# Attention and the first token products issued from one written list of small steps; q's decay table and the identity made on the chip

## The chip, the cores and the metric

The kernel runs on one core of one Trainium2 chip. The metric is the time of one execution on the device in microseconds (us), the median of three runs. A profiled execution of the same program gives the trace; its times are counted from its first instruction.

## What is computed

Three layers follow each other. Only the first and the beginning of the second are touched by the change. The shapes are batch 2, 8 heads, 768 tokens, head size 64, model width 512.

```
# attention with decay, per batch and head
for t in range(768):
    state = gamma[h] * state + outer(k[t], v[t])
    y[t]  = scale * q[t] @ state
x = y with the heads side by side            # [2, 768, 512]

# second layer
theta = x @ w_theta
zr, zi = x * cos(theta), x * sin(theta)
u = x + einsum("ts,bsd->btd", w_tok_r, zr) + einsum("ts,bsd->btd", w_tok_i, zi)
x = u + relu(u @ w_ch)

# third layer: a token MLP (w_tok1, w_tok2) and a channel MLP (w_ch1, w_ch2), each with relu and a residual
```

The weights come as float64 and are turned into float32 on the chip.

## The kernel before

**Tiling.** The 768 tokens are six chunks of 128 (c = 0 to 5), for two batches (b = 0, 1). All tiles are 128 partitions by 512 floats (256 KiB) and come from one list of 82 slots in on-chip memory.

**Attention of a chunk.** `scores(b, c)` multiplies k and q (tiles kT, qT) into banks 0 to 3 of PSUM on TensorE (PE). `masked` multiplies these by the decay mask on VectorE (DVE): two instructions to each batch, into tiles A. `intra` multiplies A by v (tile kv) into two banks of 4, 5 and 6; it opens the bank's sums with b = 0. `inter` adds q with its decay (qs) times the state. `decayed` makes qs from qT and the table qtab, and ks from k (another kv tile) and the table tabs, one DVE instruction each. `keep_x` copies the result out of PSUM on ScalarE (ACT): a rounded half xh, and the exact x into the tile X. `rest` subtracts xh in PSUM with a matrix `minus` (a negated identity), and ACT copies the remainder xl. `grow` adds ks times v to the state's sums in bank 7, and `spread` scales them into the next state on ACT.

**Weights.** `Weights` converts a 512 KiB tile in three steps. `begin` is two short DVE instructions on the loaded tile (raw) and one on ACT. `join` is one DVE instruction and one on ACT (wh). `end` is one DVE instruction (wl). Four raw tiles are in flight: a `join` sends for the next load. `theta_part(b, c, j)` is three matmuls of 128x512 with one quarter of w_theta; four of them make a theta tile. `angle`, `sines` and `turned` make cos and sin of theta on ACT and DVE, turn X on PE against the identity, and multiply and split (zh, zl). `tok(b, s, ...)` adds token chunk s to all the sums: 24 matmuls of 128x512, and 24 of 128x256.

**Order.** The program is in manual order: each engine runs its instructions in the order in which the code issues them. All loads go through the queue of SyncE (SP). Attention runs chunk by chunk (`attend`, `summed`). The theta products of chunks 0 to 2 of batch 0 stand between the scores and the intra products of chunk 4, with the conversion steps of w_theta. Chunks 4 and 5 of q, k and v are loaded behind w_theta and two tiles of w_tok. Then a loop over n = 0 to 11 does, for each (b, s), `tok` and the preparation of later tiles.

Of the kernel before, what the change touches and what calls it, by code (L numbers as in the profile page):

```python
# [8 lines left out]
F32 = mybir.dt.float32  # L9
# [46 lines left out]
            self.free_ids.append(i)  # L56


@with_exitstack
def body(ctx, tc, qk, kv, mask, tabs, qtab, ident_in, w_theta, w_tok, w_ch, w_tok1, w_tok2, w_ch1, w_ch2, out):  # L60
    nc = tc.nc
    NCH = 6
    const = ctx.enter_context(tc.tile_pool(name="const", bufs=1))
# [16 lines left out]
    def warm(n):  # L80

        for i in range(n):
            o = banks[7].rearrange("p (a b) -> p a b", a=4)
            nc.tensor.matmul(o, still, still.unsqueeze(1).to_broadcast([P, 4, P]), start=True, stop=True)
# [6 lines left out]
    magic = const.tile([P, 1], F32, name="magic")  # L91
    minus = const.tile([P, P], F32R, name="minus")

    X = const.tile([P, 3, 4, W], F32, name="X")
    nc.gpsimd.memset(half_pi, math.pi / 2)
    nc.gpsimd.memset(magic, MAGIC)

# [100 lines left out]
            return self.done[i : i + n]  # L198


    raw_t = {}

    def load_qk(b, c, parts=1):
        t = [sl.get(F32, n) for n in ("qT", "kT")]
        for i in range(parts):
            pp = slice(i * W // parts, (i + 1) * W // parts)
            for j in range(2):
                nc.sync.dma_start(out=t[j][:, pp], in_=qk[b, c, j][:, pp])  # L208
        raw_t[b, c] = t

    def load_kv(b, c, j):
        t = sl.get(F32, "kv")
        nc.sync.dma_start(out=t, in_=kv[b, c, j])
        raw_t[b, c].insert(2 + 2 * j, t)

    def load_att(b, c):
        load_qk(b, c)
        for j in range(2):
            load_kv(b, c, j)

    xs, z = {}, {}
    S, A, Q, K, V, Y, PS, R = {}, {}, {}, {}, {}, {}, {}, {}
    YS = [4, 5, 6]
    halves = [slice(64 * half, 64 * half + 64) for half in range(2)]

    def scores(b, c):

        qT, kT = raw_t[b, c][:2]
        ps = S[b, c] = banks[2 * b : 2 * b + 2]
        for p in range(4):  # L230
            pp = slice(p * P, (p + 1) * P)
            for half, r in enumerate(halves):
                nc.tensor.matmul(ps[half][:, pp], kT[r, pp], qT[r, pp], start=True, stop=True)  # L233
        let_go(b, c)

    def let_go(b, c):

        if (b, c) in V:
            sl.put(*raw_t.pop((b, c))[:3])
        else:  # L240
            V[b, c] = raw_t[b, c][3]

    def masked(b, c):
        A[b, c] = []
        for ps, m in zip(S.pop((b, c)), mask_sb):
            at = sl.get(F32, "A")
            nc.vector.tensor_mul(at, ps, m)
            A[b, c].append(at)

    def decayed(b, c):  # L250

        qT, _, k, _ = raw_t[b, c]
        if c:
            qs = sl.get(F32, "qs")
            nc.vector.tensor_mul(qs, qT, qtab_sb)
            Q[b, c] = qs
        if c < NCH - 1:
            ks = sl.get(F32, "ks")
            k3 = k.rearrange("p (h d) -> p h d", h=8)
            kt = tabs_sb[:, c, 0:8].unsqueeze(2).to_broadcast([P, 8, 64])  # L260
            nc.vector.tensor_mul(ks.rearrange("p (h d) -> p h d", h=8), k3, kt)
            K[b, c] = ks
        let_go(b, c)

# [11 lines left out]
    def third(c):  # L278

        return next(i for i in YS if all(banks[i] is not y for y in chunk(c)))  # L280
# [16 lines left out]
    def intra(b, c):  # L297
        y, a, v = chunk(c), A.pop((b, c)), V[b, c]
        for p in (0, 2, 1, 3):
            for half in range(2):  # L300
                i, ro, cc = place(b, p, half)
                hh = slice((2 * p + half) * 64, (2 * p + half + 1) * 64)
                first = b == 0 and p < 2
                nc.tensor.matmul(y[i][ro, cc], v[:, hh], a[half][:, p * P : (p + 1) * P], start=first, stop=True, skip_group_check=True)
        sl.put(*a)
# [14 lines left out]
    def rest(c):  # L320

        for i in range(2):
            hi, y = xs[c][i]
            nc.tensor.matmul(y, minus, hi, start=False, stop=True, skip_group_check=True)  # L324
            lo = sl.get(name="xl")
            nc.scalar.copy(lo, y)
            xs[c][i] = hi, lo
# [32 lines left out]
    def theta(b, c, wt, to):  # L360

        for j in range(4):
            theta_part(b, c, j, wt[j], to)
# [441 lines left out]
        nc.sync.dma_start(out=mask_sb[i], in_=mask[:, i].rearrange("p a t -> p (a t)"))  # L805
    for b in BOTH:
        load_kv(b, 0, 1)
    for b in BOTH:
        load_qk(b, 1)
    nc.sync.dma_start(out=tabs_sb, in_=tabs)  # L810
    for b in BOTH:
        load_kv(b, 0, 0)
    nc.sync.dma_start(out=ident, in_=ident_in)
    for b in BOTH:
        load_kv(b, 1, 1)
    nc.sync.dma_start(out=qtab_sb, in_=qtab)
    for b in BOTH:
        load_kv(b, 1, 0)
    for c in (2, 3):
        for b in BOTH:  # L820
            load_qk(b, c)
        for b in BOTH:
            for j in range(2):
                load_kv(b, c, j)
    for _ in range(4):
        ws.fetch()
    scores(0, 0)
    scores(1, 0)
    warm(6)
    for b in BOTH:  # L830
        masked(b, 0)
    intra(0, 0)
    warm(1)
    intra(1, 0)

    def attend(c, first, then, last):

        keep_x(c)
        first()
        for b in BOTH:  # L840
            decayed(b, c + 1)
            scores(b, c + 1)
        for b in BOTH:
            masked(b, c + 1)
        then()
        rest(c)
        grow(c)
        spread(c)
        last()

    def summed(c):
        for b in BOTH:
            intra(b, c)
        inter(c)

    def nothing():
        pass

    keep_x(0)
    for b in BOTH:  # L860
        scores(b, 1)
    for b in BOTH:
        decayed(b, 0)
    for b in BOTH:
        masked(b, 1)
    nc.scalar.activation(out=minus, in_=ident, func=AF.Copy, scale=-1.0)
    rest(0)
    grow(0)
    spread(0)
    for b in BOTH:  # L870
        decayed(b, 1)
    summed(1)
    attend(1, nothing, nothing, nothing)
    for b in BOTH:
        load_att(b, 4)
    summed(2)
    attend(2, nothing, nothing, lambda: ws.begin())
    ws.begin()
    ws.join()
    summed(3)  # L880
    ws.begin()
    ws.join()
    ws.end()
    attend(3, nothing, nothing, lambda: ws.begin())
    for b in BOTH:
        load_att(b, 5)
    for j in range(4):
        for i in range(3):
            theta_part(0, i, j, ws.done[j], (3, 2, third(4))[i])
            if j == 3:  # L890
                angle(0, i)
        if j < 2:
            ws.join()
        if j < 3:
            ws.end()
        if j == 1:
            ws.begin()
        if j == 2:
            ws.join()
            ws.begin()  # L900
            ws.end()
    wth = ws.done[0:4]
    sines(0, 0)
    summed(4)
    attend(4, nothing, nothing, nothing)
    turned(0, 0, third(5))
    ws.join()
    ws.begin()
    ws.end()
    summed(5)  # L910
    keep_x(5)
    theta(0, 3, wth, 7)
    sines(0, 1)
    ws.join()
    wtok = {0: ws.take(TOK, 3)}
    sl.put(*mask_sb, *state, qtab_sb)
    rest(5)
    grow(5)
    ws.begin()
    angle(0, 3)  # L920
    turns = [(b, c) for b in BOTH for c in range(NCH)]

    for n, (b, s) in enumerate(turns):
        tok(b, s, wtok[s], range(0, 4))
        if n:
            if n < 11:
                sines(*turns[n + 1])
            if n + 1 < NCH:
                wtok[n + 1] = ws.take(TOK + 3 * n + 3, 3)
        else:  # L930
            ws.join()
            ws.begin()
        if n < 11:
            turned(*turns[n + 1], 7)
        if n < 8:
            theta(*turns[n + 4], wth, 6)
        tok(b, s, wtok[s], range(4, 8))
        if n < 8:
            angle(*turns[n + 4])
        if n == 7:  # L940
            for x in wth:
                sl.put(*x)
        if n == 0:
            wtok[1] = ws.take(TOK + 3, 3)
        if n == NCH - 1:
            evac_u(0)
        if b:
            for x in wtok[s]:
                sl.put(*x)
            ws.pump((3, 3, 2, 2, 4, 2)[s])  # L950
        if n == 10:
            split_x(0)
# [103 lines left out]
    down_both()  # L1056


_INS = ["qk", "kv", "mask", "tabs", "qtab", "ident", "w_theta", "w_tok", "w_ch", "w_tok1", "w_tok2", "w_ch1", "w_ch2"]


def _order():
# [8 lines left out]
def _layout(q, k, v, moe_w_theta, moe_w_tok_r, moe_w_tok_i, moe_w_ch, moe2_w_tok1, moe2_w_tok2, moe2_w_ch1, moe2_w_ch2):  # L1071
# [27 lines left out]
    st = st[:, None].repeat(D, axis=1).reshape(P, n, 4)  # L1099
    arr["tabs"] = np.concatenate([kt, st], axis=2).astype(np.float32)  # L1100

    qt = (gamma[:, None] ** t[None, :] * scale).reshape(4, 2, P).transpose(1, 0, 2)
    arr["qtab"] = np.ascontiguousarray(qt[:, None].repeat(D, axis=1).reshape(P, W)).astype(np.float32)
    arr["ident"] = np.eye(P, dtype=np.float32)

    def two(a, b):

# [32 lines left out]
```

## Time and profile before

| | |
|---|---|
| median of three runs | 450.27 us (450.26 to 450.79) |
| the profiled execution | 451.72 us, span 449.9 us |
| mean granted TensorE clock | 0.992 of full speed |
| PE busy | 438.0 us of the span, 97% |
| DVE busy | 352.0 us, 78% |
| ACT busy | 228.8 us, 51% |

PE is busy nearly always, but the mean hides where it is not. The first 45 us have most of its idle time, and the one stretch in which the clock is below full speed. A time in the trace that stands in square brackets is the idle time of the engine ahead of that row, with what ended it.

### The profile page before, as it was taken

What the parts mean: (1) busy time and instruction counts of PE and PEld (TensorE: products, weight loads), DVE (VectorE), ACT (ScalarE), POOL (GpSimd) and SP (SyncE); (2) the same over time, 40 slices, a digit from 0 to 9 for tenths busy, and PEclk for the clock granted to TensorE, in tenths of its full rate; (3) what the DMA queues carried; (4) which work ended last, traced back from release to release, by engine and by line L of the source; (5) the groups of instructions that cost most, each with busy time, mean ns of one, the idle gap of its engine ahead of it and who ended that gap; (6) DMA issues with size and microseconds to landing.
All of it is one profiled execution on the core that took longest, in us unless ns stands there. A gap on an engine that the chain in (4) does not pass through costs nothing.

```text
span 449.9 us, 7132 instructions
## 1 busy us (share of the span) xinstructions
PE 438.0 (97%) x2668; PEld 367.3 (82%) x2668; DVE 352.0 (78%) x648; ACT 228.8 (51%) x411; POOL 0.3 (0%) x6
## 2 busy tenths in 40 slices
PE   7897999999999999999999999999999999999997
PEld 4775878788888888888888888888888888888886
DVE  2688776888826678899976699999878997777892
ACT  1565686677633556545534245557534545566110
POOL 0000000000000000000000000000000000000000
PEclk9996999999999999999999999999999999999999
DMA  8999512544400232374541513678220002978022
GB/s 274 385 395 390 183 48 95 176 172 142 159 8 0 95 138 96 107 255 134 204 142 45 190 60 99 228 246 265 87 94 0 2 0 70 364 269 281 0 95 93
DMA packets 36034, 68.46 MB, mean 152 GB/s; under 512 B 4128, under 2 KB 15776, under 8 KB 36000
## 3 DMA queue, kind: packets, MB, share of 16 engines
q1 hardware_dynamic: 35424, 67.10, 43.1%
q10 hardware_dynamic: 576, 0.92, 0.6%
q8 instruction: 21, 0.34, 0.3%
q14 instruction: 13, 0.11, 0.1%
HBM read 53.84 MB, written 14.16 MB: 151 GB/s over the span
## 4 chain that ended last, share of the span: by engine, by line
PE 86%; DMA 8%; ACT 2%; DVE 2%; issue 1%; SPq 1%; ACTq 0%
PE bank L112 28%; PE bank L113 28%; PE bank L114 27%; DMA kT<-in_qk 4%; DMA kv<-in_kv 2%; DMA raw<-in_w_theta 2%; PE bank L459 1%; PE bank L385 1%; PE bank L339 1%; SPq L208 1%; PE bank L324 0%; PE bank L233 0%; DVE ta L370 0%; ACT X L317 0%; ACT xh L312 0%
## 5 line engine op out<-in xcount | busy, mean ns | idle before, releaser
L113 PE MATMUL bank<-wl,zh 128*128 128x512 f32 (+1 forms) x192 | 64.9, 338 | 0.5 <-DVE wl L176 0.5
L112 PE MATMUL bank<-wh,zh 128*128 128x512 f32 (+1 forms) x192 | 64.8, 338 | 0.0
L114 PE MATMUL bank<-wh,zl 128*128 128x512 f32 (+1 forms) x192 | 64.6, 336 | 0.0
L144 ACT ACTIVATE f<-raw 128x512 f32<-128x512 f32 x56 | 37.5, 679 | 34.7 <-DVE raw L143 31.2
L154 DVE SCALAR_TENSOR_TENSOR f<-f,raw 128x512 uint32<-128x512 uint32 x56 | 38.4, 685 | 6.4 <-ACT f L144 6.4
L113 PEld LDWEIGHTS bank<-wl,zh 128*128 128x128 f32 x192 | 36.4, 190 | 4.9 <-DVE wl L176 1.3
L112 PEld LDWEIGHTS bank<-wh,zh 128*128 128x128 f32 x192 | 36.4, 190 | 3.8
L114 PEld LDWEIGHTS bank<-wh,zl 128*128 128x128 f32 x192 | 36.4, 189 | 3.8
L112 PE MATMUL bank<-uh,wh 128*128 128x512 f32 x96 | 37.4, 390 | 0.0
L113 PE MATMUL bank<-ul,wh 128*128 128x512 f32 x96 | 37.4, 389 | 0.0
L114 PE MATMUL bank<-uh,wl 128*128 128x512 f32 x96 | 37.4, 389 | 0.0
L113 PE MATMUL bank<-gl,a 128*128 128x512 f32 (+1 forms) x90 | 33.7, 375 | 0.0
L114 PE MATMUL bank<-gh,a 128*128 128x512 f32 (+1 forms) x90 | 33.7, 375 | 0.0
L112 PE MATMUL bank<-gh,a 128*128 128x512 f32 (+1 forms) x90 | 33.7, 375 | 0.0
L112 PE MATMUL bank<-bh,ah 128*128 128x512 f32 x84 | 32.7, 389 | 0.0
L113 PE MATMUL bank<-bl,ah 128*128 128x512 f32 x84 | 32.7, 389 | 0.0
L114 PE MATMUL bank<-bh,al 128*128 128x512 f32 x84 | 32.7, 389 | 0.0
L161 ACT CAST wh<-f 128x512 fp32r<-128x512 f32 x28 | 17.4, 622 | 15.4 <-DVE f L154 15.2
L143 DVE TENSOR_SCALAR raw<-raw 128x512 f32<-128x512 f32 x56 | 23.5, 420 | 2.2 <-DMA raw<-in_w_ch 2.0
L388 DVE TENSOR_TENSOR tb<-bank,tb 128x512 f32<-128x512 f32 x12 | 8.3, 689 | 20.3 <-PE bank L385 13.8
L145 DVE TENSOR_SCALAR raw<-raw 128x512 uint32<-128x512 uint32 x56 | 23.6, 422 | 0.0
L176 DVE TENSOR_TENSOR wl<-f,wh 128x512 fp32r<-128x512 f32 x28 | 19.3, 689 | 3.8 <-ACT wh L161 3.2
(132 smaller groups left out, 984.7 us busy)
## 6 DMA issues: line engine op xcount, KB each, us to landing
raw<-in_w_ch SPq DMA_DIRECT2D x28, 512.0 KB, 4.2
raw<-in_w_tok SPq DMA_DIRECT2D x24, 512.0 KB, 3.8
kv<-in_kv SPq DMA_DIRECT2D x24, 256.0 KB, 5.8
a<-keep_s SPq DMA_DIRECT2D x24, 256.0 KB, 5.3
a<-keep_a SPq DMA_DIRECT2D x18, 256.0 KB, 4.8
keep_s<-ah SPq DMA_DIRECT2D x24, 128.0 KB, 1.8
keep_s<-al SPq DMA_DIRECT2D x24, 128.0 KB, 1.8
qT<-in_qk SPq DMA_DIRECT2D x11, 256.0 KB, 5.8
```

Of the source, the lines that this page charges most:

```text
L112: nc.tensor.matmul(o, ah, bh, start=first, stop=False, skip_group_check=True)
L113: nc.tensor.matmul(o, ah, bl, start=False, stop=False, skip_group_check=True)
L114: nc.tensor.matmul(o, al, bh, start=False, stop=last, skip_group_check=True)
L143: nc.vector.tensor_scalar(out=upper, in0=upper, scalar1=MOST, scalar2=-MOST, op0=ALU.min, op1=ALU.max)
L144: nc.scalar.activation(out=f, in_=upper, func=AF.Prelu, scale=REBIAS, alpha=-SIGN)
L145: nc.vector.tensor_scalar(out=lower, in0=lower, scalar1=29, scalar2=None, op0=ALU.logical_shift_right)
L154: nc.vector.scalar_tensor_tensor(out=fu, in0=fu, scalar=3, in1=lower, op0=ALU.logical_shift_left, op1=ALU.bitwise_or)
L161: nc.scalar.copy(h, f)
L176: nc.vector.tensor_sub(l, f, h)
L208: nc.sync.dma_start(out=t[j][:, pp], in_=qk[b, c, j][:, pp])
L339: nc.tensor.matmul(o, ks[:, hh], v[:, hh], start=(b == 0 and c == 0 and p == 0), stop=True, skip_group_check=True)
L388: nc.vector.tensor_mul(u, pn, u)
```

## The change

1. A table `ORDER` of small steps (one batch of one chunk each) replaces the chunk functions, the theta block and the first three turns of the loop: attention, conversion steps, theta products and `tok` for token chunks 0 to 2 stand in it. The loop starts at turn `BEGUN` = 3. The theta products now stand behind the last attention product.
2. `decayed` becomes `decayed_q` and `decayed_k`, which are placed apart.
3. The loads stand ahead of all work, in another order. All of chunk 4 comes before w_theta. Two tiles of w_theta come before chunk 5 and two behind it. k of chunk 5 in its natural layout, which nothing reads, isn't loaded.
4. The table qtab (256 KiB) isn't loaded. Two rows of 128 and 512 floats (qrow) come through ACT's queue, one matmul spreads them over 128 partitions into bank 7, and ACT copies the result.
5. The identity (64 KiB) isn't loaded. GpSimd (POOL) makes it with a memset and a select.
6. Of seven fill matmuls on a zero tile (`warm`) beside the first scores two stay.

```
+ORDER = [
+    ('mk', 0, 0), ('ia', 0, 0), ('mk', 1, 0), ('ia', 1, 0), ('sc', 0, 1), ('dq', 0, 1), ('dk', 0, 0), ('kx', 0),
...
+    ('j',), ('an', 1, 0),
+]
+BEGUN = 3
...
+    qrows = [sl.get(F32, "qrow") for _ in range(2)]
+    nc.scalar.dma_start(out=qrows[0][0:2, 0:P], in_=qtab[:, 0:P])
+    nc.scalar.dma_start(out=qrows[1][0:2], in_=qtab[:, P:])
...
+    nc.gpsimd.memset(ident, 0.0)
+    nc.gpsimd.affine_select(
+        out=ident, in_=ident, compare_op=ALU.not_equal, fill=1.0, base=0, pattern=[[-1, P]], channel_multiplier=1
+    )
...
+    def decayed_q(b, c):
+        qs = Q[b, c] = sl.get(F32, "qs")
+        nc.vector.tensor_mul(qs, raw_t[b, c][0], qtab_sb)
+        read(b, c)
+
+    def decayed_k(b, c):
+        k, ks = KN.pop((b, c)), sl.get(F32, "ks")
...
-    for b in BOTH:
-        load_qk(b, 1)
+    load_qk(0, 1)
     nc.sync.dma_start(out=tabs_sb, in_=tabs)
     for b in BOTH:
         load_kv(b, 0, 0)
-    nc.sync.dma_start(out=ident, in_=ident_in)
-    for b in BOTH:
-        load_kv(b, 1, 1)
-    nc.sync.dma_start(out=qtab_sb, in_=qtab)
-    for b in BOTH:
-        load_kv(b, 1, 0)
-    for c in (2, 3):
+    load_qk(1, 1)
+    for j in (1, 0):
+        for b in BOTH:
+            load_kv(b, 1, j)
+    for c in range(2, NCH):
+        if c == NCH - 1:
+            ws.fetch()
+            ws.fetch()
         for b in BOTH:
             load_qk(b, c)
-        for b in BOTH:
-            for j in range(2):
+        for j in (1, 0) if c < NCH - 1 else (1,):
+            for b in BOTH:
                 load_kv(b, c, j)
-    for _ in range(4):
-        ws.fetch()
+    ws.fetch()
+    ws.fetch()
...
+    steps = dict(
+        sc=scores, mk=masked, dq=decayed_q, dk=decayed_k, ia=intra, ir=inter, kx=keep_x, re=rest, gr=grow, sp=spread,
+        b=ws.begin, j=ws.join, e=ws.end, an=angle, si=sines, tu=turned, tk=token, wa=warm,
+        th=lambda b, c, j, to: theta_part(b, c, j, wth[j], to),
+    )
     scores(0, 0)
+    nc.scalar.activation(out=minus, in_=ident, func=AF.Copy, scale=-1.0)
     scores(1, 0)
-    warm(6)
...
+    warm(2)
+    nc.tensor.matmul(banks[7], qrows[0][0:2, 0:P], qrows[1][0:2], start=True, stop=True)
+    nc.scalar.copy(qtab_sb, banks[7])
+    sl.put(*qrows)
+    for name, *args in ORDER:
+        steps[name](*args)
...
-    for n, (b, s) in enumerate(turns):
+    wtok[BEGUN] = ws.take(TOK + 3 * BEGUN, 3)
+    for n, (b, s) in list(enumerate(turns))[BEGUN:]:
         tok(b, s, wtok[s], range(0, 4))
...
```

How the instructions stand now is seen at three places. The first is SP's queue around the loads of w_theta. Before, where qT_435 is q of chunk 4 in batch 0 and qT_671 that of chunk 5:

```order
L119 DMA raw<-in_w_theta 128x1024 x4
L208 DMA qT_435<-in_qk 128x512
L208 DMA kT_436<-in_qk 128x512
L213 DMA kv_439<-in_kv 128x512
L213 DMA kv_441<-in_kv 128x512
L208 DMA qT_443<-in_qk 128x512
L208 DMA kT_444<-in_qk 128x512
L213 DMA kv_447<-in_kv 128x512
L213 DMA kv_449<-in_kv 128x512
L119 DMA raw<-in_w_tok 128x1024 x2
L208 DMA qT_671<-in_qk 128x512
L208 DMA kT_672<-in_qk 128x512
```

Now, where kv_233 and kv_235 are k of chunk 4 and qT_241 is q of chunk 5 in batch 0:

```order
L249 DMA kv_233<-in_kv 128x512
L249 DMA kv_235<-in_kv 128x512
L155 DMA raw<-in_w_theta 128x1024 x2
L244 DMA qT_241<-in_qk 128x512
L244 DMA kT_242<-in_qk 128x512
L244 DMA qT_245<-in_qk 128x512
L244 DMA kT_246<-in_qk 128x512
L249 DMA kv_249<-in_kv 128x512
L249 DMA kv_251<-in_kv 128x512
L155 DMA raw<-in_w_theta 128x1024 x2
L155 DMA raw<-in_w_tok 128x1024 x18
```

All of chunk 4 has moved ahead of w_theta, and chunk 5 ahead of half of it and of every tile of w_tok.

The second place is DVE's list around chunk 3. Before (qs_489 and ks_491 are q and k of chunk 3 in batch 0, and A_513 to A_519 the masked scores of that chunk):

```order
L255 TENSOR_TENSOR qs_489<-qT_199,qtab_99 128x512
L261 TENSOR_TENSOR ks_491<-kv_207,tabs_sb 128x512
L255 TENSOR_TENSOR qs_501<-qT_203,qtab_99 128x512
L261 TENSOR_TENSOR ks_503<-kv_211,tabs_sb 128x512
L247 TENSOR_TENSOR A_513<-bank_71,mask_97 128x512
L247 TENSOR_TENSOR A_515<-bank_72,mask_98 128x512
L247 TENSOR_TENSOR A_517<-bank_73,mask_97 128x512
L247 TENSOR_TENSOR A_519<-bank_74,mask_98 128x512
```

Now (qT_209 and qT_205 are q of chunk 3; kv_201 and kv_203 k of chunk 2; kv_217 and kv_219 k of chunk 3; A_520 to A_534 the masked scores of chunk 3):

```order
L282 TENSOR_TENSOR qs_458<-qT_209,qtab_107 128x512
L289 TENSOR_TENSOR ks_460<-kv_201,tabs_sb 128x512
L282 TENSOR_TENSOR qs_474<-qT_205,qtab_107 128x512
L289 TENSOR_TENSOR ks_484<-kv_203,tabs_sb 128x512
L289 TENSOR_TENSOR ks_508<-kv_217,tabs_sb 128x512
L289 TENSOR_TENSOR ks_510<-kv_219,tabs_sb 128x512
L271 TENSOR_TENSOR A_520<-bank_71,mask_105 128x512
L271 TENSOR_TENSOR A_522<-bank_72,mask_106 128x512
L271 TENSOR_TENSOR A_532<-bank_73,mask_105 128x512
L271 TENSOR_TENSOR A_534<-bank_74,mask_106 128x512
```

q of chunk 3 has moved ahead of k of chunk 2, and the masked scores of chunk 3 still stand behind k of that chunk, which is now the last thing loaded for it.

The third place is PE behind the first scores (bank_73 and bank_74 hold those of batch 1). Before:

```order
L233 MATMUL bank_74<-qT_150,kT_151 128x128
L84 LDWEIGHTS still
L84 MATMUL bank_78<-still 128x512
L84 LDWEIGHTS still
L84 MATMUL bank_78<-still 128x512
L84 LDWEIGHTS still
L84 MATMUL bank_78<-still 128x512
L84 LDWEIGHTS still
L84 MATMUL bank_78<-still 128x512
```

Now:

```order
L264 MATMUL bank_74<-qT_158,kT_159 128x128
L112 LDWEIGHTS still
L112 MATMUL bank_78<-still 128x512
L112 LDWEIGHTS still
L112 MATMUL bank_78<-still 128x512
L870 MATMUL bank_78<-qrow_94,qrow_93 128x512
L332 MATMUL bank_76<-A_278,kv_164 64x128
```

Four of the six fill matmuls are gone, and the matmul that spreads q's table stands in their place, ahead of the first intra product.

## Rows read from the trace of the kernel before

**Rows 1.** Stretches from:to, length: PE, PEld, DVE, ACT, POOL busy; clock; DMA share; GB/s

```profile
5.00:10.00 5.00, 3.71 (x44) 2.49 (x42) 2.34 (x4) 0.00 (x0) 0.00 (x0) 1.00 1.01 350
10.00:15.00 5.00, 4.13 (x57) 3.27 (x53) 1.89 (x4) 2.36 (x5) 0.00 (x0) 1.00 1.06 388
...
35.00:40.00 5.00, 2.04 (x24) 1.88 (x26) 3.72 (x8) 3.53 (x7) 0.00 (x0) 0.82 1.05 394
40.00:45.00 5.00, 5.00 (x48) 3.91 (x47) 4.75 (x9) 1.71 (x5) 0.00 (x0) 0.50 1.04 386
...
103.64:449.90 346.26, 343.05 (x1694) 290.57 (x1693) 277.05 (x511) 166.97 (x293) 0.00 (x0) 1.00 0.38 128
```

**Rows 2.** Waits of PE, 0 to 75 us: total, times, longest

```profile
PE bank L233 <- DMA kT<-in_qk: 4.2, 4, 1.5
```

**Rows 3.** Waits of DVE, 0 to 75 us

```profile
DVE ks L261 <- DMA kv<-in_kv: 6.3, 4, 3.1
```

**Rows 4.** Chain that ended last: start, length, what

```profile
13.99 5.81 DMA kT<-in_qk
...
32.47 6.61 DMA kT<-in_qk
```

**Rows 5.** Timeline of the attention: start, length, engine, line, tiles, count

```profile
7.42 1.47 PE L84 MATMUL bank<-still 128*128 128x512 bf16 x6
...
7.63 2.60 DVE L247 TENSOR_TENSOR A<-bank,mask 128x512 f32<-128x512 f32 x4 [6.71 <-DMA mask<-in_mask]
...
14.62 0.73 PE L324 MATMUL bank<-xh,minus 128*128 128x512 f32 x2 [0.87 <-ACT minus L866]
...
28.41 2.06 PE L233 MATMUL bank<-qT,kT 64*128 64x128 f32 x32
...
31.05 1.15 PE L339 MATMUL bank<-kv,ks 128*64 128x64 f32 x32
...
32.03 1.92 PE L304 MATMUL bank<-A,kv 128*64 128x128 f32 x32
...
33.88 1.10 PE L291 MATMUL bank<-qs,state 64*64 64x128 f32 x32
...
39.12 2.08 PE L233 MATMUL bank<-qT,kT 64*128 64x128 f32 x16 [1.44 <-DMA kT<-in_qk]
```

**Rows 6.** Timeline of PE, 45 to 105 us

```profile
45.36 0.39 PE L112 MATMUL bank<-wh,xh 128*128 128x512 f32 x1
...
52.62 0.39 PE L114 MATMUL bank<-wh,xl 128*128 128x512 f32 x1
...
62.71 1.10 PE L291 MATMUL bank<-qs,state 64*64 64x128 f32 x32
...
91.96 0.40 PE L112 MATMUL bank<-wh,zh 128*128 128x512 f32 x1
...
97.43 0.60 PE L385 MATMUL bank<-ident,X 128*128 128x128 f32 x4
...
103.48 0.40 PE L112 MATMUL bank<-wh,zh 128*128 128x512 f32 x1
```

**Rows 7.** Chain that ended last, 50 to 65 us: angle, sines, splitting

```profile
51.74 0.70 ACT ta L369
...
56.11 0.61 ACT ta L378
...
60.99 0.70 DVE tb L388
...
62.36 0.64 DVE zl L393
```

**Rows 8.** Timeline of DVE: the two short instructions of `begin`

```profile
64.18 0.42 DVE L143 TENSOR_SCALAR raw<-raw 128x512 f32<-128x512 f32 x1
64.51 0.42 DVE L145 TENSOR_SCALAR raw<-raw 128x512 uint32<-128x512 uint32 x1
```

**Rows 9.** DMA issues, 0 to 75 us: count, KB each, us to landing

```profile
tabs_sb<-in_tabs SPq DMA_DIRECT2D x1, 36.0 KB, 5.1
```

More of the change, by code (lines that the diff above doesn't have):

```diff
@@ L56, in put, with body @@
             self.free_ids.append(i)
+ORDER = [
[22 rows of a table added]
+]
+BEGUN = 3
 @with_exitstack
-def body(ctx, tc, qk, kv, mask, tabs, qtab, ident_in, w_theta, w_tok, w_ch, w_tok1, w_tok2, w_ch1, w_ch2, out):
+def body(ctx, tc, qk, kv, mask, tabs, qtab, w_theta, w_tok, w_ch, w_tok1, w_tok2, w_ch1, w_ch2, out):
     nc = tc.nc
@@ L198, in take @@
             return self.done[i : i + n]
-    raw_t = {}
+    raw_t, V, KN, readers = {}, {}, {}, {}
     def load_qk(b, c, parts=1):
@@ L213, in load_kv @@
         nc.sync.dma_start(out=t, in_=kv[b, c, j])
-        raw_t[b, c].insert(2 + 2 * j, t)
-    def load_att(b, c):
-        load_qk(b, c)
-        for j in range(2):
-            load_kv(b, c, j)
+        (V if j else KN)[b, c] = t
     xs, z = {}, {}
-    S, A, Q, K, V, Y, PS, R = {}, {}, {}, {}, {}, {}, {}, {}
+    S, A, Q, K, Y, PS, R = {}, {}, {}, {}, {}, {}, {}
     YS = [4, 5, 6]
@@ L233, in scores @@
                 nc.tensor.matmul(ps[half][:, pp], kT[r, pp], qT[r, pp], start=True, stop=True)
[L234 to L241, printed above, removed]
+        read(b, c)
     def masked(b, c):
@@ L248, in masked, with read @@
             A[b, c].append(at)
[L250 to L263, printed above, removed]
+    def read(b, c):
+        readers[b, c] = readers.get((b, c), 0) + 1
+        if readers[b, c] == (2 if c else 1):
+            sl.put(*raw_t.pop((b, c)))
+    def decayed_q(b, c):
+        qs = Q[b, c] = sl.get(F32, "qs")
+        nc.vector.tensor_mul(qs, raw_t[b, c][0], qtab_sb)
+        read(b, c)
+    def decayed_k(b, c):
+        k, ks = KN.pop((b, c)), sl.get(F32, "ks")
+        k3 = k.rearrange("p (h d) -> p h d", h=8)
+        kt = tabs_sb[:, c, 0:8].unsqueeze(2).to_broadcast([P, 8, 64])
+        nc.vector.tensor_mul(ks.rearrange("p (h d) -> p h d", h=8), k3, kt)
+        K[b, c] = ks
+        sl.put(k)
     def place(b, p, half):
@@ L812, in body @@
         load_kv(b, 0, 0)
-    nc.sync.dma_start(out=ident, in_=ident_in)
-    for b in BOTH:
-        load_kv(b, 1, 1)
-    nc.sync.dma_start(out=qtab_sb, in_=qtab)
-    for b in BOTH:
-        load_kv(b, 1, 0)
-    for c in (2, 3):
+    load_qk(1, 1)
[6 more added lines that the diff above has]
+            ws.fetch()
         for b in BOTH:
             load_qk(b, c)
-        for b in BOTH:
-            for j in range(2):
+        for j in (1, 0) if c < NCH - 1 else (1,):
+            for b in BOTH:
@@ L824, in body, with token @@
                 load_kv(b, c, j)
-    for _ in range(4):
-        ws.fetch()
+    ws.fetch()
+    ws.fetch()
+    wth, wtok = ws.done, {}
+    def token(b, s, half):
+        wtok[s] = ws.done[TOK + 3 * s : TOK + 3 * s + 3]
+        tok(b, s, wtok[s], range(4 * half, 4 * half + 4))
+    steps = dict(
[3 more added lines that the diff above has]
+    )
@@ L827, in body @@
     scores(0, 0)
+    nc.scalar.activation(out=minus, in_=ident, func=AF.Copy, scale=-1.0)
     scores(1, 0)
-    warm(6)
[L830 to L901, printed above, removed]
@@ L902, in body @@
-    wth = ws.done[0:4]
[L903 to L920, printed above, removed]
+    warm(2)
+    nc.tensor.matmul(banks[7], qrows[0][0:2, 0:P], qrows[1][0:2], start=True, stop=True)
+    nc.scalar.copy(qtab_sb, banks[7])
@@ L921, in body @@
+    sl.put(*qrows)
+    for name, *args in ORDER:
+        steps[name](*args)
+    sl.put(*mask_sb, *state, qtab_sb)
+    wth = ws.done[0:4]
     turns = [(b, c) for b in BOTH for c in range(NCH)]
-    for n, (b, s) in enumerate(turns):
+    wtok[BEGUN] = ws.take(TOK + 3 * BEGUN, 3)
+    for n, (b, s) in list(enumerate(turns))[BEGUN:]:
         tok(b, s, wtok[s], range(0, 4))
[L925 to L932, printed above, removed]
+        if n < 11:
+            sines(*turns[n + 1])
+        if n + 1 < NCH:
+            wtok[n + 1] = ws.take(TOK + 3 * n + 3, 3)
@@ L942, in body @@
                 sl.put(*x)
-        if n == 0:
-            wtok[1] = ws.take(TOK + 3, 3)
         if n == NCH - 1:
@@ L1056, in body @@
     down_both()
-_INS = ["qk", "kv", "mask", "tabs", "qtab", "ident", "w_theta", "w_tok", "w_ch", "w_tok1", "w_tok2", "w_ch1", "w_ch2"]
+_INS = ["qk", "kv", "mask", "tabs", "qtab", "w_theta", "w_tok", "w_ch", "w_tok1", "w_tok2", "w_ch1", "w_ch2"]
 def _order():
@@ L1100, in _layout @@
     arr["tabs"] = np.concatenate([kt, st], axis=2).astype(np.float32)
-    qt = (gamma[:, None] ** t[None, :] * scale).reshape(4, 2, P).transpose(1, 0, 2)
-    arr["qtab"] = np.ascontiguousarray(qt[:, None].repeat(D, axis=1).reshape(P, W)).astype(np.float32)
-    arr["ident"] = np.eye(P, dtype=np.float32)
+    qt = (gamma[:, None] ** t[None, :] * scale).reshape(4, 2, P).transpose(1, 0, 2).reshape(2, W)
+    arr["qtab"] = np.concatenate([np.eye(2).repeat(D, axis=1), qt], axis=1).astype(np.float32)
     def two(a, b):
```

20 rows, old and new, of the table ORDER are left out of this document.

## The prediction

> **What bounds the kernel now.** I read the busy time by stretches first, then the waits of PE and DVE, then the chain that ended last, then the timeline. From 103.64 us to the end PE is busy for 343.05 of 346.26 us [rows 1]. Nothing that the change touches can shorten that part, and whatever comes earlier at its start should come earlier at its end. So the whole question is when the token products of turn 3 begin: at 103.48 us before [rows 6]. Ahead of it three things cost time. PE waits for q and k of the scores, 4.2 us in four waits [rows 2]. In the stretch from 35 to 40 us PE is busy for only 2.04 of 5 us, and the granted clock falls to 0.82 and then 0.50, which is the 1.2 GHz level, up to 45 us [rows 1]. The chain agrees: it runs over loads of kT, one of which lands at 13.99 + 5.81 = 19.80 us, another at 32.47 + 6.61 = 39.08 us [rows 4]. The second is k of chunk 4, which stands in SP's list behind all of w_theta. The loads run at 386 to 394 GB/s there [rows 1], so the early part is bound by the order and the amount of the loads, the rest of it by the order of the steps.
>
> **The loads.** In SP's list of before, q and k of chunk 2 in batch 0 end after 5,476 KiB, and q and k of chunk 4 in batch 1 after 12,644 KiB. These two landings give 19.28 us for 7,168 KiB, 2.69 us for each 1,000 KiB (381 GB/s). The change removes 512 KiB (k of chunk 5), 256 KiB (the table) and 64 KiB (the identity): 832 KiB or 2.2 us of loading. Counting the new list from the same anchor: k of chunk 3 is complete after 8,740 KiB, at 19.8 + 3.264 x 2.69 = 28.6 us; q and k of chunk 4 after 9,764 KiB, at 31.3 us instead of 39.1; q and k of chunk 5 after 12,836 KiB, at 39.6 us; its v after 13,348 KiB, at 41.0 us.
>
> The Trainium skill (DMA: Bandwidth & Descriptors, Specifications) gives a limit of about 358 GB/s for what HBM delivers to one core. The rows stand above it, so the measurement decides; by the page's figure k of chunk 3 would land 0.6 us later and the gain below would be 6.3 instead of 6.9 us, an estimate.
>
> **The new attention.** At full clock a chunk takes PE 2.06 us for the scores of both batches, 1.92 for intra, 1.10 for inter, 1.15 for grow and 0.73 for rest [rows 5]. DVE needs 2.60 us for four masked tiles, that is 0.62 each when they follow one another [rows 5]; I take 0.62 for each full-size DVE instruction and 0.33 for the short ones [rows 8]. Up to chunk 3 the loads pace everything. DVE then stands before k of chunk 3 (28.6), with the masked scores of chunk 3 queued behind it: the last ks ends at 29.3, four masked tiles at 31.8, intra of the second batch at 33.0 with 0.2 us of handing over, inter at 34.1. From here q and k are already on the chip, and a chunk repeats with a period: scores 2.06, then 1.9 until the last masked tile (the scores of one batch are masked while the other's run; rest and grow, 0.73 + 1.15, fill this gap on PE), 0.1 of handing over, intra 1.92, inter 1.10: 7.1 us. Two periods, chunks 4 and 5, end the attention at 34.1 + 14.2 = 48.3 us. Loads don't delay them: q and k of chunk 5 (39.6) are wanted at 41.2, its v (41.0) at 45.
>
> **From there to turn 3.** What is left of PE's list up to turn 3: 48 theta matmuls at (52.62 - 45.36) / 32 = 0.227 us, 10.9 us; the rest of chunk 5, 0.7; the first transposes, 0.6 [rows 5, 6]; three turns of tokens, transposes and theta at 103.48 - 91.96 = 11.52 us each [rows 6], 34.6. Sum 46.8 us. Without a further wait turn 3 begins at 95.1 us.
>
> **The waits W on the way** are the unknown. The first token products want zh and zl of chunk 0. Its theta ends 24 matmuls or 5.4 us behind the attention, at 53.7. The way through angle and sines took 56.72 - 51.74 = 5.0 us before, of which 1.2 went into two other angles; products and splitting took 63.00 - 60.99 = 2.0 us [rows 7]; with 1.9 us of weight steps that now stand between, the tile is ready at 61.4. PE gets there at 53.7 + 0.7 + 0.6 + 30 x 0.227 = 61.8: no wait, with little to spare. Behind it DVE's own load is the measure: between the last masked tile (45.3 us) and the second weight tile of token chunk 2 its list holds 41 full and 26 short instructions, 41 x 0.62 + 26 x 0.33 = 34.0 us, so it could be there at 79.3, and PE wants it at about 48.3 + 10.9 + 1.3 + 23.0 = 83.5. Lower bound of W: 0. Upper bound: DVE loses as large a share as it did in the stretch from 35 to 45 us of before, where it was busy for 8.47 of 10 us [rows 1]; 34.0 becomes 40.1 us, and it is there at 85.4; with one more wait as long as the longest for k, 3.1 us [rows 3], at 88.5. W is 0 to 5.0 us. I take 1.5, nearer to the lower end, since the list spreads the weight steps between the other work and 4 us of slack come first.
>
> **Small edits.** The two qrow loads are issued on ACT's queue in the first 2 us; the slowest small load took 5.1 us [rows 9], so they are there by about 6.3, while PE comes to their matmul at 7.9, behind the scores and two fill matmuls. That matmul has no row of its own: bounds 0.2 us (half of a theta matmul's place) and 0.73 (two of rest, [rows 5]); it lies in the gap up to the first masked tiles at 8.9 [rows 5], where six fill matmuls took 1.47 us. Cost 0; if the gap were gone, 0.7. The copy of the table on ACT must end by 10.2, when DVE wants it. The identity on POOL has no row near it (its memsets of one column are short); it is wanted by ACT ahead of that copy, so it has some 8 us, and costs nothing below that. It takes away the 0.87 us by which rest of chunk 0 waited for `minus` [rows 5], but the loads pace that part anyway.
>
> **Sum.** 48.3 + 46.8 + 1.5 = 96.6 us against 103.48: 6.9 us earlier. The profiled execution took 451.72 us, so 444.8 for one like it; the median of the runs is 1.45 below the profiled one, which gives 443.4 us.
>
> **The rivals.** *DVE gives part of it back* (W at its upper bound): turn 3 at 100.1, gain 3.4, 446.9 us. For it: 34 us of DVE work in a stretch of 38, all in one fixed order, with links over ACT in between. The Trainium skill (TensorE: Matmul & The Clock Gate, Architectural detail) says that ACT and DVE run strictly in order; the waits for k agree, 6.3 us in which the masked scores queued behind. Against it: 4 us of slack.
>
> *No change.* The list puts q or k of a later chunk ahead of masked scores. If each of chunks 3 to 5 holds DVE for 1.1 us more than I have, the attention ends 3.4 us later, and with 5.0 us of W the gain of 8.4 - W is gone: 450.3 us. Against it: from chunk 4 on the data are early by my landings.
>
> *Slower, by the clock.* Five of seven fill matmuls go, some 1.2 us of 7.84 us that PE was busy from 5 to 15 us at full clock [rows 1]. If the clock falls there, each chunk takes twice its PE time: 16 score instructions took 2.08 us at the low level, 32 took 2.06 at the full one [rows 5]. A low stretch costs half its busy length, so from 13.8 us on it costs more than 6.9; 20 us would give 450.3 - 6.9 + 10.0 = 453.4 us. Against it: 3.71 busy of 5 kept the clock at 1.00, and it fell only after 2.04 of 5, a hole that the new order of loads fills. The Trainium skill (TensorE: Matmul & The Clock Gate, Part 1) says that the throttled clock is the default and that activity releases it, which is the rule against dropping fill matmuls; by it this rival would come true if the first chunk's holes were deep enough.
>
> *More.* W is 0 and the attention ends 1 us earlier, since the first chunks gain from the shorter loads too: gain 9.4, 440.9 us.
>
> **How the numbers follow.** A change under 0.2% (0.9 us) can't be told from none here. Forecast (gain 5 to 9.3, 441.0 to 445.3 us) 0.58; DVE rival (gain 1 to 5) 0.22; no change 0.06; slower 0.06; more 0.08. The low end is the attention 1 us earlier without W (440.9, set to 440.8); the high end, 448.0, takes in the greater part of the DVE rival, and about 2 in 10 are left out. Faster 0.88, same 0.06, slower 0.06.
>
> **What the profile after would show.** Loads: k of chunk 4's scores no longer in PE's waits, and no stretch near 40 us at 0.50. Attention: the last inter ends near 48 us, followed by theta matmuls without a hole. Then turn 3's first 128x512 token matmul near 96.6 us; behind it PE as full as before. I am wrong if inter of chunk 5 ends behind 52 us (loads or DVE's order), if PE waits more than 4 us for DVE between 48 and 97 us, or if the clock falls below 1.00 between 10 and 48 us.

## The result, and the profile after

The changed kernel took 442.78 us in the median of four runs (442.6 to 444.09), the kernel before 450.37 us beside it. The ratio is 0.9836 with a 95% interval of 0.9816 to 0.9856: 7.6 us faster, where 6.9 us and 443.4 us were forecast. A second set of runs of the same kernel, with the kernel before beside it again, gave 442.68 us and 0.9821 [0.9802, 0.9840].

The stretches of the changed kernel stand below, in the columns of [rows 1].

```profile
5.00:10.00 5.00, 4.42 (x31) 3.09 (x30) 1.75 (x3) 0.00 (x0) 0.00 (x0) 1.00 0.98 298
10.00:15.00 5.00, 4.81 (x52) 3.29 (x52) 3.12 (x6) 3.01 (x6) 0.00 (x0) 1.00 1.06 392
...
35.00:40.00 5.00, 5.00 (x98) 4.30 (x92) 4.85 (x9) 3.60 (x7) 0.00 (x0) 1.00 1.03 392
40.00:45.00 5.00, 4.70 (x86) 3.85 (x82) 4.22 (x9) 4.22 (x11) 0.00 (x0) 1.00 0.91 344
...
49.62:95.90 46.28, 46.28 (x247) 39.77 (x246) 39.70 (x78) 34.18 (x60) 0.00 (x0) 1.00 0.45 160
...
95.90:442.30 346.40, 343.38 (x1697) 290.96 (x1696) 278.04 (x512) 166.92 (x294) 0.00 (x0) 1.00 0.38 130
```

The hole at 35 to 45 us and its clock of 0.82 and 0.50 [rows 1] are gone. From the end of the attention to turn 3 PE is never idle. Behind the beginning of turn 3 the changed kernel takes 442.3 - 96.07 = 346.2 us, the one before 449.9 - 103.48 = 346.4 us: that part only moved.

PE's waits from 0 to 100 us, against 4.2 us for kT alone before [rows 2]:

```profile
PE bank L264 <- DMA kT<-in_qk: 1.0, 2, 0.6
PE bank L112 <- DVE still L106: 1.0, 1, 1.0
PE bank L352 <- ACT X L345: 0.7, 2, 0.5
PE bank L332 <- DVE A L271: 0.2, 1, 0.2
```

The timeline of the changed kernel at the places that the prediction names: the first scores and the table's matmul, ks of chunk 3 on DVE, the last inter, the first theta matmul, the first token matmul of turn 3.

```profile
4.08 2.08 PE L264 MATMUL bank<-qT,kT 64*128 64x128 f32 x16
...
9.72 1.35 PE L870 MATMUL bank<-qrow,qrow 2*128 2x512 f32 x2
...
29.46 1.36 DVE L289 TENSOR_TENSOR ks<-kv,tabs_sb 128x512 f32<-128x512 f32 x2 [0.26 <-DMA kv<-in_kv]
...
48.52 1.10 PE L319 MATMUL bank<-qs,state 64*64 64x128 f32 x32
49.56 0.50 PE L148 MATMUL bank<-wh,xh 128*128 128x512 f32 x1
...
96.07 0.40 PE L148 MATMUL bank<-wh,zh 128*128 128x512 f32 x1
```

The attention ends at 49.62 us (48.3 were forecast), and turn 3 begins at 96.07 us (96.6 forecast; 103.48 before [rows 6]). The 7.4 us between are nearly all of the 7.6 us by which the two profiled executions differ (451.72 and 444.09).

### The profile page after: what moved, and what is told of

It is laid out like the page before. It is cut to its first block, busy times and chain, and to the rows that moved or that the text cites. A ratio compares the mean times of both kernels' runs of the same rounds, so it can differ in the third digit from the quotient of the medians.

```text
span 442.3 us, 7135 instructions
## 1 busy us (share of the span) xinstructions
PE 436.3 (99%) x2665; PEld 367.3 (83%) x2665; DVE 351.1 (79%) x648; ACT 228.4 (52%) x412; POOL 0.8 (0%) x8
## 4 chain that ended last, share of the span: by engine, by line
PE 89%; DMA 6%; DVE 1%; SPq 1%; ACT 1%; issue 1%; DVEq 0%; ACTq 0%
PE bank L148 29%; PE bank L150 29%; PE bank L149 29%; DMA kv<-in_kv 5%; DMA kT<-in_qk 1%; PE bank L413 1%; PE bank L487 1%; SPq L244 1%; DVE A L271 1%; PE bank L332 0%; ACT state L376 0%; PE bank L367 0%; ACT xh L340 0%; PE bank L319 0%; PE bank L352 0%
## 5 line engine op out<-in xcount | busy, mean ns | idle before, releaser
L533 ACT CAST ah<-s 128x512 fp32r<-128x512 f32 x24 | 14.3, 618 | 14.2 <-DVE s L618 9.5
```

The lines of the kernel that those rows point to most:

```text
L533: nc.scalar.copy(h[:, 0:n], f)
```

## The experiments

Theory 1 is the prediction's: the order of the loads and the list of steps carry the gain, and behind the attention DVE has slack. Its rivals: the list alone, the bytes alone, the small edits at the start, or DVE as a hidden bound. Each ratio is to the kernel before on the same chip. Of ratios between two variants I use differences only where they are clear of the intervals, which are 0.2 to 0.3% to either side.

| kernel | median us | ratio [95%] |
|---|---|---|
| changed kernel again (e0) | 442.68 | 0.9821 [0.9802, 0.9840] |
| its list, w_theta loaded first (e1) | 447.35 | 0.9910 [0.9881, 0.9939] |
| k of chunk 5 loaded again (e2) | 444.12 | 0.9845 [0.9815, 0.9875] |
| table and identity loaded again (e3) | 443.56 | 0.9829 [0.9801, 0.9857] |
| new list, old loads (e4) | 448.88 | 0.9951 [0.9933, 0.9970] |
| before, fewer loads (e5) | 449.43 | 0.9973 [0.9957, 0.9990] |
| old list, new loads (e6) | 457.79 | 1.0154 [1.0134, 1.0175] |
| six fill matmuls (e7) | 442.56 | 0.9835 [0.9806, 0.9863] |
| eight more DVE steps (e8) | 447.27 | 0.9926 [0.9902, 0.9951] |
| sixteen more (e9) | 455.15 | 1.0081 [1.0052, 1.0111] |
| before, holes filled (e10) | 450.32 | 0.9980 [0.9964, 0.9996] |
| eight more, later (e11) | 445.91 | 0.9872 [0.9845, 0.9899] |

**The changed kernel again.** No edit. Expected: 

> The changed kernel itself, beside the next three on one chip, as their reference. Theory and rival alike: a ratio to the kernel before of 0.982 to 0.985; the time at which PE reaches its full rate at the start may differ from the first profile, the end of the attention by less than 1 us.

Measured 442.68 us. Its profile shows how far one execution may differ from the next at the start:

```profile
4.08 1.98 PE L264 MATMUL bank<-qT,kT 64*128 64x128 f32 x16
6.78 1.16 PE L264 MATMUL bank<-qT,kT 64*128 64x128 f32 x16 [0.72 <-DMA kT<-in_qk]
...
28.46 1.38 DVE L289 TENSOR_TENSOR ks<-kv,tabs_sb 128x512 f32<-128x512 f32 x2 [0.65 <-DMA kv<-in_kv]
...
46.83 1.10 PE L319 MATMUL bank<-qs,state 64*64 64x128 f32 x32
47.86 0.50 PE L148 MATMUL bank<-wh,xh 128*128 128x512 f32 x1
...
94.38 0.40 PE L148 MATMUL bank<-wh,zh 128*128 128x512 f32 x1
```

Here the second 16 score instructions take 1.16 us; in the first profile both groups took 2.08, and its attention ends 1.7 us later. That first profiled execution is the 444.09 of the four runs, this one took 442.42. So the first profile shows an unlucky execution, and the expectation of less than 1 us was too narrow. The late start is only a part of the 1.7 us: its loads ran slower from 25 to 35 us as well (see *Loads* below).

**w_theta first.** The four loads of w_theta stand ahead of chunk 4 again.

```
     for c in range(2, NCH):
-        if c == NCH - 1:
-            ws.fetch()
-            ws.fetch()
+        if c == NCH - 2:
+            for _ in range(4):
+                ws.fetch()
...
-    ws.fetch()
-    ws.fetch()
```

Expected: 

> The changed kernel with all four tiles of w_theta loaded ahead of chunk 4, as before the change; nothing else moves. Theory 1 (the order of the loads carries most of the gain): k of chunk 4, which DVE's list reads ahead of that chunk's masked scores, lands 2,048 KiB later, 5.5 us, so the attention ends near 54 instead of 49.6 us and the time is 446.5 to 448.5 us. Rival (the list of steps carries it, the loads have slack): at most 1 us slower, 442.8 to 443.8 us.

Measured 447.35 us, as theory 1 had it. The scores of chunk 4 wait for their loads, DVE then for ks, and the clock falls in the hole. This kernel's timeline of PE, of DVE, and the stretch (columns of [rows 1]):

```profile
37.04 3.37 PE L264 MATMUL bank<-qT,kT 64*128 64x128 f32 x32 [2.62 <-DMA kT<-in_qk]
```

```profile
36.26 0.69 DVE L282 TENSOR_TENSOR qs<-qT,qtab 128x512 f32<-128x512 f32 x1 [4.02 <-DMA qT<-in_qk]
38.96 1.45 DVE L289 TENSOR_TENSOR ks<-kv,tabs_sb 128x512 f32<-128x512 f32 x2 [2.01 <-DMA kv<-in_kv]
```

```profile
35.00:40.00 5.00, 2.96 (x28) 2.99 (x30) 1.67 (x3) 1.51 (x4) 0.00 (x0) 0.66 1.05 386
```

By the ratios this is 3.3 to 4.0 us slower than the changed kernel, by the medians 4.6. The rival (the list has slack against the loads) is out.

**The bytes.** k of chunk 5 loaded again behind its v (`for j in (1, 0):` for all chunks); then, by itself, the table and the identity loaded ahead of q and k of chunk 1, with the two qrow loads, their matmul and POOL's steps taken out:

```
+    nc.sync.dma_start(out=ident, in_=ident_in)
+    nc.sync.dma_start(out=qtab_sb, in_=qtab)
     load_qk(0, 1)
...
-    nc.tensor.matmul(banks[7], qrows[0][0:2, 0:P], qrows[1][0:2], start=True, stop=True)
-    nc.scalar.copy(qtab_sb, banks[7])
```

Expected: 

> The changed kernel with k of chunk 5 loaded again behind its v (512 KiB that nothing reads). Theory 1: only loads ahead of chunk 4's k pace the attention; this one stands behind what is waited for, delays two tiles of w_theta by 1.4 us, and costs 0 to 0.3 us: 442.7 to 443.1 us. Rival (every byte removed is time): 1.4 us slower, 444.2 us.

Expected: 

> The changed kernel with q's table and the identity loaded again (320 KiB, behind v of chunk 0) instead of made on the chip. Theory 1: q, k and v from chunk 1 on land 0.86 us later; the matmul that spreads the table (1.35 us in the profile) goes; the scores of chunk 2 are the first thing that the loads still hold, so 0.4 to 0.9 us slower, 443.2 to 443.7 us. Rival (making the table costs as much at the start as its load): no difference, 442.6 to 443.0 us.

The first is unclear: 1.4 us above the changed kernel by the medians of two chips, 0.1 to 0.2% by the ratios, which overlap. The second is unclear too: its ratio lies between the two of the changed kernel, as its rival had it, its median of 443.56 us where theory 1 had it, and the interval of 0.28% (1.3 us) to either side takes in both. What making the table could gain is small in any case: its matmul is two instructions of 1.35 us together in the first profile and 1.12 us in the second, ahead of the first intra product, beside 0.86 us of loading.

**New list on the old loads.** The two edits above and w_theta first together. The old order is not restored in full: chunk 5 still stands ahead of w_tok, v ahead of k, and the table and the identity stand ahead of chunk 1.

Expected: 

> The list of steps of the changed kernel on the loads of before: w_theta ahead of chunk 4, k of chunk 5, table and identity loaded. Theory 1: as with w_theta first, and 0.9 us more: 447 to 449.5 us, so the list alone gains 1 to 3 us. Rival (the list carries the gain): 443.5 to 445 us.

Measured 448.88 us: 0.5% faster than before, 2.2 us, within the expected 1 to 3. On these loads the list gives less than a third of the gain.

**Fewer loads in the kernel before.** Its order is kept; k of chunk 5, table and identity aren't loaded, and four fill matmuls and the table's matmul stand where six fill matmuls stood.

```
-        for j in range(2):
+        for j in range(2) if c < NCH - 1 else (1,):
             load_kv(b, c, j)
...
-    nc.sync.dma_start(out=ident, in_=ident_in)
...
-    nc.sync.dma_start(out=qtab_sb, in_=qtab)
```

Expected: 

> The kernel before, its list and order of loads kept, but without the 832 KiB of loads: no k of chunk 5, table and identity made on the chip. Theory 1 (it is the order, not the amount): 320 KiB stand ahead of chunk 2, so q and k of chunk 4 land 0.9 us earlier; gain 0.3 to 1.5 us, ratio 0.997 to 0.9995. Rival (the bytes carry the gain): 2.2 us or more, ratio under 0.995.

Measured 0.9973, 1.2 us (0.5 to 1.9 by the interval), as theory 1 had it: the bytes alone are a small part.

**Old list on the new loads.** The loads of the changed kernel in amount and order, ahead of all steps, with the steps of before (`load_att(b, 4)` and `load_att(b, 5)` are gone from their places) and the fill matmuls and the table's matmul of the variant just above.

Expected: 

> The list of steps of before on the loads of the changed kernel (amount and order). q and k of chunk 4 are there at 31 us, but two tiles of w_theta land behind chunk 5, near 44 us, and the old list has DVE's begin of the third tile and the theta block ahead of the rest of chunk 4. Theory 1 (loads and list need each other): no gain, 449 to 453 us, ratio 0.997 to 1.006. Rival (the loads alone give the gain, the list only follows): ratio under 0.99.

Measured 457.79 us, 1.5% slower than before, beyond the forecast. DVE and PE of this kernel:

```profile
43.09 0.43 DVE L151 TENSOR_SCALAR raw<-raw 128x512 f32<-128x512 f32 x1 [4.55 <-DMA raw<-in_w_theta]
...
43.56 0.69 ACT L152 ACTIVATE f<-raw 128x512 f32<-128x512 f32 x1 [4.35 <-DVE raw L151]
...
45.03 0.57 ACT L322 CAST xh<-bank 128x512 fp32r<-128x512 f32 x1
...
46.14 0.80 PE L334 MATMUL bank<-xh,minus 128*128 128x512 f32 x1 [6.91 <-ACT X L327]
```

The third tile of w_theta now lands behind chunk 5. DVE stands before it for 4.55 us, ACT behind DVE, and ACT's `keep_x` of chunk 3 stands in ACT's list behind that weight step; so PE waits 6.91 us for a copy whose data had long been there, and goes on at the low clock (0.80 us for a 128x512 matmul). The better order of loads is a loss for the old list.

**Fill matmuls.** `warm(6)` instead of `warm(2)`.

Expected: 

> The changed kernel with six fill matmuls beside the first scores instead of two. Theory 1: the loads of chunks 1 and 2 pace what follows, so 0 to 0.6 us slower than the changed kernel beside it. Rival (dropping fill matmuls cost clock at the start): 0.5 us faster or more.

Measured 442.56 us and a ratio between the two of the changed kernel: no difference that these runs can tell.

**DVE's slack.** Eight or sixteen more multiplications of a 128x512 tile that nothing else uses, in two halves, `('ex', 4)` or `('ex', 8)` ahead of `('tk', 0, 0, 0)` and behind `('an', 0, 4)`; then eight at one place behind `('an', 0, 5)`. They are work that the reference doesn't have.

Expected: 

> The changed kernel with eight more full-size DVE multiplications on a tile that nothing else uses (about 5 us): four ahead of the first token products, four ahead of the second half of token chunk 1. Theory (DVE has about 4 us of slack between the attention and turn 3, so its load costs nothing now): 0 to 1.5 us slower than the changed kernel's 442.7 us. Rival (DVE paces this stage and the waits of PE only don't show): about 5 us slower, 447 to 448 us.

Expected: 

> The same with sixteen, eight at each place (about 9.9 us). Theory: beyond the slack of 4 us nearly all of it shows: 4 to 7 us slower than 442.7 us, with PE waiting for DVE between 50 and 100 us. Rival (the slack is larger than DVE's idle time suggests): under 2 us.

Expected: 

> The changed kernel with the same eight DVE multiplications (5 us) at one later place, behind the angle of chunk 5, ahead of token chunk 2's second half. Theory (the slack depends on the place: there DVE waits for PE again, 1.7 and 1.3 us): 1 to 2.5 us slower than 442.7 us. Rival (no slack anywhere): 4.5 us slower, as with eight at the two earlier places.

Each multiplication holds DVE for 0.7 us, so eight are 5.6 us and sixteen 11.4, not the 5 and 9.9 of the expectations. The theory fell for the two early places: eight cost 4.0 to 4.7 us (0.9926 against 0.9821 and 0.9836), close to what the rival had. At the later place the same work cost 1.6 to 2.3 us, as expected of a place where DVE waits. PE's waits in the kernel with eight, then in the one with sixteen, with a stretch of the latter (columns of [rows 1]):

```profile
73.25 0.65 PE L413 MATMUL bank<-ident,X 128*128 128x128 f32 x4 [1.09 <-DVE ta L416]
75.23 0.50 PE L149 MATMUL bank<-wl,zh 128*128 128x512 f32 x1 [0.40 <-DVE wl L212]
87.01 0.51 PE L148 MATMUL bank<-wh,zh 128*128 128x512 f32 x1 [0.66 <-ACT wh L197]
88.50 0.50 PE L149 MATMUL bank<-wl,zh 128*128 128x512 f32 x1 [0.99 <-DVE wl L212]
```

```profile
75.79 1.12 PE L413 MATMUL bank<-ident,X 128*128 128x128 f32 x4 [4.08 <-DVE ta L416]
...
89.87 0.50 PE L149 MATMUL bank<-wl,zh 128*128 128x512 f32 x1 [0.59 <-DVE wl L212]
...
92.46 0.63 PE L148 MATMUL bank<-wh,zh 128*128 128x512 f32 x1 [1.86 <-ACT wh L197]
...
93.95 0.80 PE L149 MATMUL bank<-wl,zh 128*128 128x512 f32 x1 [0.86 <-DVE wl L212]
```

```profile
48.00:100.00 52.00, 44.61 (x205) 36.42 (x202) 46.97 (x89) 32.17 (x56) 0.00 (x0) 0.90 0.38 134
```

The first eight of the sixteen on DVE:

```profile
66.96 5.78 DVE L825 TENSOR_TENSOR idle<-idle 128x512 f32<-128x512 f32 x8
```

The first wait of each kernel is that of a chunk's transposes for the bank that DVE has still to read, the others are for weight tiles of token products. Without the extra work PE waits at none of these places. Sixteen cost 11.0 to 11.7 us, far beyond the 4 to 7 that were expected and as much as the added work holds DVE. PE's four waits are 7.4 us of it; the mean clock of the stretch is 0.90, and the work behind the holes runs slower.

**The clock in the holes of before.** Six fill matmuls into a free bank ahead of each of the two score groups of chunk 4, in the kernel before.

```
         for b in BOTH:
             decayed(b, c + 1)
+            if c == 3:
+                warm(6, 4)
             scores(b, c + 1)
```

Expected: 

> The kernel before with six fill matmuls ahead of each of the two score groups of chunk 4, in the holes in which PE waits for their loads; they keep PE busy and compute nothing. Theory (a part of what the change gains is the clock that fell in those holes; the work from 39 to 45 us took some 2.7 us longer at the low level): PE at its full rate there, 1.5 to 3 us faster than the kernel before, ratio 0.993 to 0.997. Rival (the low clock is hidden behind DVE and the loads): no difference.

The clock stayed at full speed, the scores took 1.16 us instead of 2.08 [rows 5], and the gain was 0.9 us (0.9980), between the two expectations. Two rows of its PE timeline and a stretch (columns of [rows 1]), then a piece of its chain that ended last (start, length, what):

```profile
39.69 1.16 PE L233 MATMUL bank<-qT,kT 64*128 64x128 f32 x16
...
43.48 0.50 PE L112 MATMUL bank<-wh,xh 128*128 128x512 f32 x1 [0.88 <-DVE A L247]
```

```profile
40.00:45.00 5.00, 4.12 (x57) 3.21 (x54) 4.66 (x9) 3.12 (x8) 0.00 (x0) 1.00 1.04 388
```

```profile
34.30 6.01 DMA kv<-in_kv
...
40.34 0.63 DVE ks L261
40.96 2.47 DVE A L247 x4
...
43.48 0.50 PE bank L112
```

The chain goes from the load over ks and the masked scores to theta and passes by PE. The chain of the kernel before did pass through PE's work at the low level:

```profile
39.12 2.08 PE bank L233 x16
41.20 1.15 PE bank L324 x2
42.35 1.91 PE bank L339 x32
```

With that work at full speed PE waits 0.88 us for DVE instead, and turn 3 begins at 102.50 us in this profile, 1.0 us earlier than before. So of the 2.7 us by which the low clock made PE's work longer, 1.0 us shows between these two profiles; another part lay beside a load and DVE steps that were nearly as long.

The 0.9 us is an average over unlike executions. The kernel before ran 65 times beside the variants. In 25 of these the mean granted clock is 0.999 or more, and their median is 450.2 us; in 18 it is 0.992 or less, as in the profile of before, and their median is 452.4 us. All twelve executions with the holes filled have 0.999 or more, with a median of 450.3 us. So an execution of before that kept its clock had nothing to gain, and one whose clock fell was some 2 us longer. Whether the clock makes up all of these 2 us isn't shown.

## Why the prediction was right

- *Loads.* k of chunk 3 was put at 28.6 us; ks starts at 29.46 in the first profile and at 28.46 in the second. The order of the loads was named as the cause, and w_theta first takes 3.3 to 4.6 us of the gain back. The loads of the first profile were 0.12 MB behind those of the second at 25 us, after a slower stretch from 5 to 10 us (298 GB/s, in the second profile 335), and 0.34 MB behind at 30 us. The stretches from 25 us, two of the first profile and one of the second:

```profile
25.00:30.00 5.00, 5.00 (x107) 4.54 (x102) 3.04 (x6) 3.20 (x8) 0.00 (x0) 1.00 1.00 341
30.00:35.00 5.00, 4.78 (x89) 3.68 (x89) 4.00 (x8) 2.12 (x6) 0.00 (x0) 1.00 1.02 362
```

```profile
25.00:30.00 5.00, 5.00 (x106) 4.27 (x102) 4.03 (x7) 2.05 (x4) 0.00 (x0) 1.00 1.05 384
```

Why they ran slower in that one execution isn't known. The 358 GB/s that the Trainium skill gives as a limit (DMA: Bandwidth & Descriptors, Specifications) lies below the 384 of the second profile, as it did below the rows of before from 10 us on, and above the 341 of the first. The second profile, with k of chunk 3 at 28.46, bears out the forecast's own rate of 381 GB/s.
- *Attention.* The end at 48.3 us: 49.62 and 47.93. In the second profile the chain that ended last is the forecast one, from the load of k of chunk 3 over ks and the masked scores to PE, which then runs through. Its periods, from the end of one inter to the end of the next, are 6.84 and 6.68 us instead of 7.1. In the first profile they are 6.82 and 7.41; that their sum is the forecast 14.2 us is luck, since the second one holds waits for the steps of ACT and DVE. One load was left out of the forecast. It took q and k of chunk 4 to be on the chip at 31.3 us, but the k that ks reads comes behind v, and DVE waits for it in both profiles, here the first and then the second:

```profile
34.82 1.35 DVE L289 TENSOR_TENSOR ks<-kv,tabs_sb 128x512 f32<-128x512 f32 x2 [1.00 <-DMA kv<-in_kv]
```

```profile
33.86 1.35 DVE L289 TENSOR_TENSOR ks<-kv,tabs_sb 128x512 f32<-128x512 f32 x2 [1.02 <-DMA kv<-in_kv]
```

Only in the first profile does the chain go over this load.
- *The rest of the list.* 46.8 us were forecast; 96.07 - 49.56 = 46.51 and 94.38 - 47.86 = 46.52 were measured.
- *W.* 1.5 us were taken, between 0 and 5.0; it is 0 in both profiles. This is the term that was mis-sized. In the first profile an attention that ends 1.3 us later, W less by 1.5 us and a list shorter by 0.3 us leave turn 3 0.5 us ahead of the forecast; in the second all three are shorter and it is 2.2 us ahead (94.38 against 96.6). That the medians differ from the forecast by only 0.7 to 1.1 us of gain is in part luck: the gain was counted from a profile of before in which the clock had fallen, and was taken off a median 1.45 us below it. The reason that I gave for a small W, 4 us of slack, was wrong. DVE was to have the second weight tile of token chunk 2 at 79.3 us and PE to want it at 83.5. In the first profile DVE ends it at 84.4 and PE reads it at 85.5, so that 1.0 us of slack was left:

```profile
83.14 1.29 DVE L212 TENSOR_TENSOR wl<-f,wh 128x512 fp32r<-128x512 f32 x2
```

```profile
85.47 0.39 PE L149 MATMUL bank<-wl,zh 128*128 128x512 f32 x1
```

From its last masked tile DVE took 37.3 us instead of the 34.0 of my count; 2.6 of the difference are its own waits for ACT and for a load, which the count left out. The added work agrees. The DVE rival was therefore nearer than its 0.22 suggested: eight more steps on DVE and half of the gain is gone.
- *The list and the loads need each other.* I argued with both at once and did not say it. The list on nearly the old loads 0.9951, the loads alone 1.0154, both 0.9821 to 0.9836.
- *What bounds the kernel.* I counted the low clock among the things that cost time before. Kept at full speed there, it gives back 0.9 us on average; in the profiles 1.0 us of the 2.7 us by which PE's work there ran longer.
- *Small edits.* The runs can't tell their cost from 0. The table's matmul took 1.12 to 1.35 us, above my upper bound of 0.73. In the second profile it was hidden: behind it PE still waits 0.27 us for v of chunk 0. POOL's identity was made by 1.3 us. The rival "slower, by the clock" did not come: six fill matmuls change nothing that can be told.

What stays open: which of the loads that went paid for how much in the new order. k of chunk 5 is within the intervals, and whether the table's load and its making cancel is too.

## What to carry to other kernels

An order of loads and an order of steps are one edit: in-order engines turn a load that has moved back into a wait of whatever is queued behind its first reader, on three engines in turn. Slack has a place: sum a helper engine's work, and its own waits, up to each product that needs it, not up to the last, and test it by adding work there, with the length of that work read from the trace. Before a low clock is counted as a loss, look for the way that is nearly as long beside it: the chain that ended last passed through the low clock, and yet a load and DVE's steps took over once it was gone.

## What the hardware showed that I had not expected

- *The rate at which PE starts differs between executions, and the clock column doesn't show it.* In the profile of before and in both profiles after, the same seven fill matmuls start at 0.98 us and the first scores at 4.08. These 16 score instructions took 1.27 us in the profile of before, 2.08 and again 2.08 for the next 16 in the first profile after, 1.98 and then 1.16 in the second. The column of the granted clock says 1.00 in all of them; 2.08 us is what [rows 5] shows at 0.50. In the first profile after the low rate lasts to about 11 us. The row of before:

```profile
4.08 1.27 PE L233 MATMUL bank<-qT,kT 64*128 64x128 f32 x16
```

- *A matmul with two rows is not cheap.* The table's, 128x512 from 2 partitions in plain float32, appears as two instructions and takes 1.12 us together at full rate, where a 128x512 matmul with all 128 rows on rounded tiles takes 0.50 us. No run here has one with all rows in plain float32 beside it.
- *A hole costs more than its length.* With sixteen extra DVE steps the way from the end of the attention to turn 3 grew by 12.7 us against the first profile after. PE's four waits are 7.4 us of that. Behind them the clock fell, and PE's own work ran longer:

```profile
75.00:80.00 5.00, 4.21 (x14) 3.55 (x15) 4.91 (x11) 3.26 (x7) 0.00 (x0) 0.66 0.47 173
...
95.00:100.00 5.00, 5.00 (x14) 3.95 (x13) 3.97 (x10) 3.06 (x6) 0.00 (x0) 0.55 0.53 192
```
